# FNet mixing and an MLP-mixer block on one core: rewriting the sine/cosine table stage, loading the first input early, and re-splitting one eviction

## The chip, the cores and the metric

One core of a Trainium2 chip runs the whole program. The metric is the device time of one execution in microseconds (us). Medians are quoted; several runs of one kernel agree within about 0.3%. The profile calls TensorE PE, its weight loads PEld, VectorE DVE, ScalarE ACT and GpSimd POOL.

## The reference, cut to what matters

```python
def _attn_ref(x):                       # x: (8, 3008, 256) float32
    X = np.fft.fft(x, axis=1)           # along the 3008 rows
    X = np.fft.fft(X, axis=2)           # along the 256 columns
    return X.real.astype(np.float32)

def _moe_ref(x, w_tok1, w_tok2, w_ch1, w_ch2):
    xt = x.transpose(0, 2, 1)
    h = np.maximum(xt @ w_tok1, 0.0) @ w_tok2          # token mixing, 3008 -> 256 -> 3008
    u = x + h.transpose(0, 2, 1)
    h2 = np.maximum(u @ w_ch1, 0.0) @ w_ch2            # channel mixing, 256 -> 1536 -> 256
    return (u + h2).astype(np.float32)
```

The Fourier transform along the rows is done as matrix products with a table of cosines and one of sines. The kernel makes these tables on the chip at its start: 24 blocks of 128 rows, 753 useful columns each (padded to 768), stored as fp16. It then treats the 8 batches one after the other.

## The kernel before: the parts that matter

Tables, pass 1: for each of 24 blocks, sine and cosine of 256 columns in fp32. Pass 2: casts to fp16, and angle addition for the other 512 columns.

```python
    def sincos(m, W, Sf, out_sin, out_cos):
        v = ...;  v = m * (1/Sf) + 2**23          # DVE
        v = v - 2**23                             # DVE: rounded quotient
        r = v * (-Sf) + m                         # DVE, two tensors: remainder
        out_sin = Sin(r * 2*pi/Sf)                # ACT
        m4 = m * 4 + Sf                           # DVE
        v2 = m4 * (1/(4*Sf)) + 2**23              # DVE
        v2 = v2 - 2**23                           # DVE
        r2 = v2 * (-Sf) + m                       # DVE, two tensors
        out_cos = Sin(r2 * 2*pi/Sf + pi/2)        # ACT
```

(The body above is abbreviated to one line per instruction; each line is one call in the kernel.)

```python
    elC = gen.tile([P, NT, 256], FP32, tag="elC", bufs=1)
    elS = gen.tile([P, NT, 256], FP32, tag="elS", bufs=1)
    for nt in range(NT):                                             # pass 1
        m = gen.tile([P, 256], FP32, tag="m256")
        nc.vector.tensor_scalar(out=m[:], in0=jrow[:], scalar1=nval[:, nt:nt + 1], ...)
        sincos(m, 256, float(S), elS[:, nt, :], elC[:, nt, :])
    for nt in range(NT):                                             # pass 2
        nc.vector.tensor_copy(out=tabC[:, nt, 0:256], in_=elC[:, nt, :])
        nc.vector.tensor_copy(out=tabS[:, nt, 0:256], in_=elS[:, nt, :])
        for q in (1, 2):
            # tmp1 = elS * ss_q (ACT);  tabC[q] = elC * sc_q - tmp1 (DVE)
            # tmp2 = elC * ss_q (ACT);  tabS[q] = elS * sc_q + tmp2 (DVE)
            ...
```

The pool of the per-batch tiles is opened after the table pool is closed, so that it takes over its memory; the input of batch 0 is loaded inside the batch loop, by 48 loads that POOL issues:

```python
    perb = ctx.enter_context(tc.tile_pool(name="perb", bufs=1))
    work = ctx.enter_context(tc.tile_pool(name="work", bufs=1))
    for b in range(BB):
        x16 = perb.tile([P, NT, D], FP16, tag="x16")
        for nt in range(NT):
            nc.gpsimd.dma_start(out=x16[0:nw, nt, :], ...)           # even rows
            nc.gpsimd.dma_start(out=x16[64:64 + nw, nt, :], ...)     # odd rows
        ...
        for mt in range(2):
            for tbl, dt_, dr in ((tabC, ATt, ATr), (tabS, BTt, BTr)):    # four DFT groups
                pe_lo = pst("pe_lo"); pe_hi = pst("pe_hi")           # 4 of 8 PSUM banks
                po_lo = pst("po_lo"); po_hi = pst("po_hi")
                for nt in range(NT):
                    # 4 matmuls: even and odd rows, columns 0:512 and 512:768 of block nt
                    ...
                # eviction: pos <- po_lo, po_hi (ACT), then eight adds and subtracts (DVE)
```

In the order of the program there are four such DFT groups a batch: group 0 (cosines, left half of the columns), 1 (sines, left), 2 and 3 (right half). The kernel's PSUM pool has eight tiles and a group takes four, so two groups can be open at once. The other place that the change touches is the eviction of the channel mixing's first product, 12 tiles to a step:

```python
                    if ct % 2 == 0:
                        nc.scalar.activation(out=c1[:, ct, :], in_=pc[:], func=AFT.Relu)
                    else:
                        nc.vector.tensor_scalar(out=c1[:, ct, :], in0=pc[:], ..., op0=AT.max)
```

## Time and profile before

| | before |
|---|---|
| time, median of the first 4 runs | 1103.73 us (1103.7 to 1104.23) |
| first matmul | 105.8 us |
| eviction of batch 0's last DFT group starts | 151.9 us |
| batch 0's last matmul ends | 242.75 us |
| one batch after that | 122.3 us |

Start with the page's picture of the span: each digit is the busy share, in tenths, of one of 40 slices of 27.6 us.

```profile
## 2 busy tenths in 40 slices
PE   0001999999999999999999999999999999999998
PEld 0000477666766666665776676666767676666765
DVE  9997176544865367535855367545755466536654
ACT  4585032321333142321323032312332033313232
POOL 2002644000800062001700062003500080000000
```

PE is idle for almost four slices and full after that; DVE is full while PE is idle. The next view gives busy time by stretches: start:end, length, then busy us (and instructions) of PE, PEld, DVE, ACT and POOL, then the recorded clock of PE, the DMA share and GB/s.

```profile
0.00:51.00 51.00, 0.00 (x0) 0.00 (x0) 49.84 (x207) 24.50 (x53) 6.88 (x16) 1.00 0.57 92
51.00:98.00 47.00, 0.00 (x0) 0.00 (x0) 47.00 (x143) 40.17 (x94) 0.00 (x0) 1.00 0.00 0
98.00:103.00 5.00, 0.00 (x0) 0.00 (x0) 4.43 (x17) 1.81 (x4) 0.29 (x1) 1.00 0.00 0
103.00:152.00 49.00, 43.56 (x386) 25.47 (x387) 11.62 (x30) 2.75 (x8) 24.85 (x48) 0.97 0.31 33
```

The four lines are pass 1, pass 2, the small tables for the column transform, and the DFT of batch 0. In the last one POOL is busy issuing the loads. The waits up to 160 us say who waited for whom, in total, how often and longest:

```profile
PE pe_lo L219 <- DMA x<-in_x_dram: 106.4, 3, 105.8
```

PE's first matmul did wait for the input, whose first load was issued at 103.6 us (the timeline puts POOL's wait before it down to ACT's last table instruction, which frees the memory). PE then follows the loads. The timeline of the ACT evictions shows when each of the four DFT groups of batch 0 was done:

```profile
131.00 0.60 ACT L228 ACTIVATE pos<-po_lo 128x512 f16<-128x512 f32 x1 [27.96 <-PE po_lo L223]
...
136.23 0.60 ACT L228 ACTIVATE pos<-po_lo 128x512 f16<-128x512 f32 x1 [4.36 <-PE po_lo L223]
...
144.08 0.60 ACT L228 ACTIVATE pos<-po_lo 128x512 f16<-128x512 f32 x1 [6.99 <-issue]
...
151.88 0.60 ACT L228 ACTIVATE pos<-po_lo 128x512 f16<-128x512 f32 x1 [6.93 <-issue]
```

The last two groups are 7.8 us apart, which is a group at PE's full rate (the four of batch 1 are 7.8 us apart too); the first two wait for loads. Finally, the chain of waits gives the batch period: the last run of channel-mixing matmuls of batch 0, and that of batch 7.

```profile
237.51 5.24 PE pc L362 x48
...
1093.43 5.25 PE pc L362 x48
```

One more reading is needed, of what an instruction costs on an engine. An instruction's duration includes latency that its successor can overlap (on DVE one of 0.28 us is followed after 0.20); what counts is the interval from start to start in a full stretch. In the table passes these intervals are, for 256 fp32 columns: DVE with one tensor 0.20 us (0.26 with a per-partition factor), DVE with two tensors 0.34 (0.40 with a per-partition factor), ACT 0.40 with a per-partition factor.

### The profile page before, as it was taken

The numbers are of one execution on the slowest core, as the hardware profiler recorded it, in microseconds if no ns is written. First come the engines' busy times: TensorE is split into PE (matmuls) and PEld (weight loads), VectorE is DVE, ScalarE is ACT, GpSimd is POOL, SyncE is SP. The second block draws the span as 40 slices with busy tenths as digits, with TensorE's granted clock in tenths as the row PEclk, the third lists the DMA queues.
The fourth block names the chain that finished last, engine by engine and source line by source line (L and its number), as shares of the span: only waits on it lengthen the run. The fifth ranks groups of instructions, "written<-read, shape, count | busy, mean of one in ns | idle before, by whom it ended". The sixth has DMA issues, their size and how long they took to land.

```text
span 1102.7 us, 20768 instructions
## 1 busy us (share of the span) xinstructions
PE 979.7 (89%) x8448; PEld 667.3 (61%) x8448; DVE 669.1 (61%) x1588; ACT 343.6 (31%) x711; POOL 203.8 (18%) x401
## 2 busy tenths in 40 slices
PE   0001999999999999999999999999999999999998
PEld 0000477666766666665776676666767676666765
DVE  9997176544865367535855367545755466536654
ACT  4585032321333142321323032312332033313232
POOL 2002644000800062001700062003500080000000
PEclk9999999999999999999999999999999999999999
DMA  9001423110511032110411032111311041100011
GB/s 168 2 0 12 45 30 48 43 52 1 58 39 57 19 38 40 55 40 11 49 53 43 19 40 46 48 38 18 41 56 54 5 51 45 45 32 1 16 43 56
DMA packets 62415, 42.99 MB, mean 39 GB/s; under 512 B 9105, under 2 KB 61808, under 8 KB 62320
## 3 DMA queue, kind: packets, MB, share of 16 engines
q0 software_dynamic: 35392, 17.01, 13.3%
q1 hardware_dynamic: 26928, 24.65, 6.7%
q8 instruction: 66, 1.08, 0.4%
q14 instruction: 29, 0.24, 0.1%
HBM read 33.98 MB, written 24.64 MB: 53 GB/s over the span
## 4 chain that ended last, share of the span: by engine, by line
PE 73%; DVE 17%; issue 7%; POOL 2%; ACT 1%; DMA 0%; DVEq 0%; ACTq 0%; POOLq 0%
PE pc L362 23%; PE pc L342 22%; PE pe_lo L219 11%; PE pe_hi L221 5%; PE pt L302 4%; PE pU L282 3%; PE pU L278 3%; DVE Yr L316 3%; DVE tabS L151 2%; DVE tabC L144 2%; DVE Yh L316 2%; DVE UTh L330 1%; DVE r L111 1%; DVE r L98 1%; POOL x L191 1%
## 5 line engine op out<-in xcount | busy, mean ns | idle before, releaser
L346 ACT ACTIVATE c<-pc 128x512 f16<-128x512 f32 x288 | 171.9, 597 | 364.5 <-PE pc L342 186.4
L362 PE MATMUL pc<-wc,c 128*128 128x256 f16 x2304 | 259.4, 273 | 0.0
L191 POOL DMA_DIRECT2D x<-in_x_dram x192 | 138.0, 718 | 613.6 <-PE po_hi L225 604.9
L362 PEld LDWEIGHTS <-c 128*128 128x128 f16 x2304 | 225.0, 98 | 36.8
L349 DVE TENSOR_SCALAR c<-pc 128x512 f16<-128x512 f32 x288 | 195.4, 690 | 51.9 <-PE pc L342 48.7
L219 PE MATMUL pe_lo<-tabC,x 64*128 64x512 f16 x384 | 129.6, 384 | 106.8 <-DMA x<-in_x_dram 106.4
L219 PEld LDWEIGHTS <-x 64*128 64x128 f16 x768 | 72.4, 94 | 195.7 <-issue 107.9
L342 PEld LDWEIGHTS <-wc 128*128 128x128 f16 x1152 | 112.2, 98 | 129.7 <-issue 5.9
L195 POOL DMA_DIRECT2D x<-in_x_dram x192 | 139.3, 726 | 2.7 <-issue 2.7
L342 PE MATMUL pc<-UTh,wc 128*128 128x512 f16 x576 | 130.8, 379 | 1.4
L223 PE MATMUL po_lo<-tabC,x 64*128 64x512 f16 x384 | 129.7, 384 | 1.7 <-DMA x<-in_x_dram 1.5
L342 PE MATMUL pc<-UTr,wc 128*128 128x512 f16 x576 | 128.2, 379 | 0.0
L219 PE MATMUL pe_lo<-tabS,x 64*128 64x512 f16 x384 | 127.1, 379 | 0.0
L223 PE MATMUL po_lo<-tabS,x 64*128 64x512 f16 x384 | 126.6, 378 | 0.0
L228 ACT ACTIVATE pos<-po_lo 128x512 f16<-128x512 f32 x32 | 19.1, 597 | 283.2 <-PE po_hi L225 139.5
L221 PE MATMUL pe_hi<-tabC,x 64*128 64x256 f16 x384 | 105.0, 273 | 0.0
L225 PE MATMUL po_hi<-tabC,x 64*128 64x256 f16 x384 | 105.0, 273 | 0.0
L221 PE MATMUL pe_hi<-tabS,x 64*128 64x256 f16 x384 | 103.8, 270 | 0.0
L225 PE MATMUL po_hi<-tabS,x 64*128 64x256 f16 x384 | 103.8, 270 | 0.0
L367 DVE TENSOR_TENSOR osb<-pc,Yr 128x256 f32<-128x256 f32 x96 | 40.7, 424 | 78.6 <-PE pc L362 78.6
L367 DVE TENSOR_TENSOR osb<-pc,Yh 128x256 f32<-128x256 f32 x96 | 40.8, 425 | 76.8 <-PE pc L362 76.8
L232 DVE TENSOR_TENSOR ATt<-pe_lo,pos 128x512 f16<-128x512 f32 x16 | 11.1, 692 | 117.8 <-ACT pos L228 117.8
(101 smaller groups left out, 1286.6 us busy)
## 6 DMA issues: line engine op xcount, KB each, us to landing
out_dram<-osb SPq DMA_DIRECT2D x176, 128.0 KB, 1.7
x<-in_x_dram POOLq DMA_DIRECT2D x368, 32.0 KB, 2.3
wc<-in_moe_w_ch_dram POOLq DMA_DIRECT2D x2, 768.0 KB, 20.6
w2f<-in_moe_w_tok_dram POOLq DMA_DIRECT2D x1, 1504.0 KB, 16.0
out_dram<-osb SPq DMA_DIRECT2D x8, 97.0 KB
w1h<-in_moe_w_tok_dram POOLq DMA_DIRECT2D x1, 768.0 KB, 7.8
out_dram<-osb SPq DMA_DIRECT2D x8, 95.0 KB
w1r<-in_moe_w_tok_dram POOLq DMA_DIRECT2D x1, 704.0 KB, 10.2
```

Of the source, the lines that this page charges most:

```text
L191: nc.gpsimd.dma_start(out=x16[0:nw, nt, :], in_=bass.AP(tensor=x_t, offset=(b * S + nt * P) * D, ap=[[2 * D, nw], [1, D]]))
L195: nc.gpsimd.dma_start(out=x16[64:64 + nw, nt, :], in_=bass.AP(tensor=x_t, offset=(b * S + nt * P + 1) * D, ap=[[2 * D, nw], [1, D]]))
L219: nc.tensor.matmul(pe_lo[:], lhsT=lhs_e, rhs=tbl[0:64, nt, 0:512], start=st, stop=sp)
L221: nc.tensor.matmul(pe_hi[:, 0:256], lhsT=lhs_e, rhs=tbl[0:64, nt, 512:KHP], start=st, stop=sp)
L223: nc.tensor.matmul(po_lo[:], lhsT=lhs_o, rhs=tbl[64:P, nt, 0:512], start=st, stop=sp)
L225: nc.tensor.matmul(po_hi[:, 0:256], lhsT=lhs_o, rhs=tbl[64:P, nt, 512:KHP], start=st, stop=sp)
L316: nc.vector.tensor_tensor(out=Yt[:, kt, :], in0=Yt[:, kt, :], in1=ph[:, 0:D], op=AT.add)
L342: nc.tensor.matmul(pc[:], lhsT=wc1[:, dt, ct * P:(ct + 1) * P], rhs=UTt[:, dt, kc * 512:(kc + 1) * 512], start=(dt == 0), stop=(dt == 1))
L346: nc.scalar.activation(out=c1[:, ct, :], in_=pc[:], func=AFT.Relu)
L349: nc.vector.tensor_scalar(out=c1[:, ct, :], in0=pc[:], scalar1=0.0, scalar2=None, op0=AT.max)
L362: nc.tensor.matmul(pc2[:, 0:D], lhsT=c1[:, ct, ks * P:(ks + 1) * P], rhs=wc2[:, ct, :], start=(ct == 0), stop=(ct == NKT - 1))
L367: nc.vector.tensor_tensor(out=osb[0:hi, :], in0=pc2[0:hi, 0:D], in1=Ut[0:hi, kt, :], op=AT.add)
```

## The change

Its intent is a shorter front. It has four parts:

1. The pool of the per-batch tiles is opened before the table pool, so that it has memory of its own, and batch 0 is loaded first.
2. The two table passes become one loop over blocks, with small buffers in place of two big ones.
3. Table arithmetic: the rounding multiply-add moves to ACT, and the cosine is made as 1 - 2 sin(x/2)^2 from the same remainder, which saves the second range reduction.
4. The channel-mixing evictions are split 8 to 4 between ACT and DVE in place of 6 to 6.

```diff
+    perb = ctx.enter_context(tc.tile_pool(name="perb", bufs=1))
+    def load_x(b):  ...                       # as in the loop before
+    x16_first = load_x(0)
     with tc.tile_pool(name="tgen", bufs=3) as gen:
@@ (cut: sincos gets a variant with multiply-adds on ACT, which no caller uses;
@@  the small tables move ahead of the loop) @@
-        elC = gen.tile([P, NT, 256], FP32, tag="elC", bufs=1)
-        elS = gen.tile([P, NT, 256], FP32, tag="elS", bufs=1)
         for nt in range(NT):
             m = ...
-            sincos(m, 256, float(S), elS[:, nt, :], elC[:, nt, :])
-        for nt in range(NT):
-            nc.vector.tensor_copy(out=tabC[:, nt, 0:256], in_=elC[:, nt, :])
-            nc.vector.tensor_copy(out=tabS[:, nt, 0:256], in_=elS[:, nt, :])
+            elC = gen.tile([P, 256], FP32, tag="elC")
+            elS = gen.tile([P, 256], FP32, tag="elS")
+            va = gen.tile([P, 256], FP32, tag="sv256")
+            nc.scalar.activation(out=va[:], in_=m[:], func=AFT.Copy,
+                                 scale=1.0 / S, bias=TWO23)
+            nc.vector.tensor_scalar(out=va[:], in0=va[:], scalar1=-TWO23, ..., op0=AT.add)
+            r = gen.tile([P, 256], FP32, tag="sr256")
+            nc.vector.scalar_tensor_tensor(out=r[:], in0=va[:], scalar=-float(S),
+                                           in1=m[:], op0=AT.mult, op1=AT.add)
+            nc.scalar.activation(out=elS[:], in_=r[:], func=AFT.Sin, scale=2 * pi / S)
+            nc.scalar.activation(out=h[:], in_=r[:], func=AFT.Sin, scale=pi / S)
+            nc.scalar.activation(out=h2[:], in_=h[:], func=AFT.Square)
+            nc.vector.tensor_scalar(out=elC[:], in0=h2[:], scalar1=-2.0,
+                                    scalar2=1.0, op0=AT.mult, op1=AT.add)
+            nc.vector.tensor_copy(out=tabC[:, nt, 0:256], in_=elC[:])
+            nc.vector.tensor_copy(out=tabS[:, nt, 0:256], in_=elS[:])
             for q in (1, 2):                  # angle addition as before
@@ (cut) @@
-    perb = ctx.enter_context(tc.tile_pool(name="perb", bufs=1))
     for b in range(BB):
-        x16 = perb.tile(...)                  # and its 48 loads
+        x16 = x16_first if b == 0 else load_x(b)
@@ (cut) @@
-                    if ct % 2 == 0:
+                    if ct % 3 != 2:
```

More of the change, by code (lines that the diff above doesn't have):

```diff
@@ L87, with load_x @@
     wc2 = const.tile([P, NKT, D], FP16, tag="wc2")
-    with tc.tile_pool(name="tgen", bufs=3) as gen:
-        def sincos(m, W, Sf, out_sin, out_cos):
-            v = gen.tile([P, W], FP32, tag=f"sv{W}")
-            nc.vector.tensor_scalar(out=v[:], in0=m[:], scalar1=1.0 / Sf,
-                                    scalar2=TWO23, op0=AT.mult, op1=AT.add)
-            nc.vector.tensor_scalar(out=v[:], in0=v[:], scalar1=-TWO23,
+    perb = ctx.enter_context(tc.tile_pool(name="perb", bufs=1))
+    def load_x(b):
+        x16 = perb.tile([P, NT, D], FP16, tag="x16")
+        nc.vector.memset(x16[:, NT - 1, :], 0.0)
+        for nt in range(NT):
+            nw = 64 if nt < NT - 1 else 32
+            nc.gpsimd.dma_start(
+                out=x16[0:nw, nt, :],
+                in_=bass.AP(tensor=x_t, offset=(b * S + nt * P) * D,
+                            ap=[[2 * D, nw], [1, D]]))
+            nc.gpsimd.dma_start(
+                out=x16[64:64 + nw, nt, :],
+                in_=bass.AP(tensor=x_t, offset=(b * S + nt * P + 1) * D,
+                            ap=[[2 * D, nw], [1, D]]))
+        return x16
@@ new lines @@
+    qjr = const.tile([P, NT * 2], FP32, tag="qjr")
+    nc.gpsimd.iota(qjr[:], pattern=[[0, NT], [256, 2]], base=256,
+                   channel_multiplier=0, allow_small_or_imprecise_dtypes=True)
+    dcols = []
+    for dt in range(2):
+        dcol = const.tile([P, 1], FP32, tag=f"dcol{dt}")
+        nc.gpsimd.iota(dcol[:], pattern=[[0, 1]], base=128 * dt,
+                       channel_multiplier=1,
+                       allow_small_or_imprecise_dtypes=True)
+        dcols.append(dcol)
@@ new lines, with sincos @@
+    x16_first = load_x(0)
+    with tc.tile_pool(name="tgen", bufs=3) as gen:
+        def sincos(m, W, Sf, out_sin, out_cos, split):
+            va = gen.tile([P, W], FP32, tag=f"sv{W}")
+            if split:
+                nc.scalar.activation(out=va[:], in_=m[:], func=AFT.Copy,
+                                     scale=1.0 / Sf, bias=TWO23)
+            else:
+                nc.vector.tensor_scalar(out=va[:], in0=m[:], scalar1=1.0 / Sf,
+                                        scalar2=TWO23, op0=AT.mult, op1=AT.add)
+            nc.vector.tensor_scalar(out=va[:], in0=va[:], scalar1=-TWO23,
@@ L96, in sincos @@
                                     scalar2=None, op0=AT.add)
             r = gen.tile([P, W], FP32, tag=f"sr{W}")
-            nc.vector.scalar_tensor_tensor(out=r[:], in0=v[:], scalar=-Sf,
+            nc.vector.scalar_tensor_tensor(out=r[:], in0=va[:], scalar=-Sf,
                                            in1=m[:], op0=AT.mult, op1=AT.add)
@@ L102, in sincos @@
             m4 = gen.tile([P, W], FP32, tag=f"sm{W}")
-            nc.vector.tensor_scalar(out=m4[:], in0=m[:], scalar1=4.0, scalar2=Sf,
-                                    op0=AT.mult, op1=AT.add)
-            v2 = gen.tile([P, W], FP32, tag=f"sw{W}")
-            nc.vector.tensor_scalar(out=v2[:], in0=m4[:], scalar1=1.0 / (4 * Sf),
-                                    scalar2=TWO23, op0=AT.mult, op1=AT.add)
-            nc.vector.tensor_scalar(out=v2[:], in0=v2[:], scalar1=-TWO23,
+            vb = gen.tile([P, W], FP32, tag=f"sw{W}")
+            if split:
+                nc.scalar.activation(out=m4[:], in_=m[:], func=AFT.Copy,
+                                     scale=4.0, bias=Sf)
+                nc.scalar.activation(out=vb[:], in_=m4[:], func=AFT.Copy,
+                                     scale=1.0 / (4 * Sf), bias=TWO23)
+            else:
+                nc.vector.tensor_scalar(out=m4[:], in0=m[:], scalar1=4.0,
+                                        scalar2=Sf, op0=AT.mult, op1=AT.add)
+                nc.vector.tensor_scalar(out=vb[:], in0=m4[:],
+                                        scalar1=1.0 / (4 * Sf), scalar2=TWO23,
+                                        op0=AT.mult, op1=AT.add)
+            nc.vector.tensor_scalar(out=vb[:], in0=vb[:], scalar1=-TWO23,
                                     scalar2=None, op0=AT.add)
             r2 = gen.tile([P, W], FP32, tag=f"sp{W}")
-            nc.vector.scalar_tensor_tensor(out=r2[:], in0=v2[:], scalar=-Sf,
+            nc.vector.scalar_tensor_tensor(out=r2[:], in0=vb[:], scalar=-Sf,
                                            in1=m[:], op0=AT.mult, op1=AT.add)
@@ L117 @@
         ss_q = const.tile([P, NT * 2], FP32, tag="ss_q")
-        qjr = gen.tile([P, NT * 2], FP32, tag="qjr", bufs=1)
-        nc.gpsimd.iota(qjr[:], pattern=[[0, NT], [256, 2]], base=256,
-                       channel_multiplier=0, allow_small_or_imprecise_dtypes=True)
         mq = gen.tile([P, NT * 2], FP32, tag="mq", bufs=1)
@@ L124 @@
         nc.vector.tensor_tensor(out=mq[:], in0=qjr[:], in1=nval_b, op=AT.mult)
-        sincos(mq, NT * 2, float(S), ss_q[:], sc_q[:])
-        elC = gen.tile([P, NT, 256], FP32, tag="elC", bufs=1)
-        elS = gen.tile([P, NT, 256], FP32, tag="elS", bufs=1)
+        sincos(mq, NT * 2, float(S), ss_q[:], sc_q[:], False)
+        for dt in range(2):
+            dcol = dcols[dt]
+            md = gen.tile([P, 256], FP32, tag="m256")
+            nc.vector.tensor_scalar(out=md[:], in0=jrow[:], scalar1=dcol[:],
+                                    scalar2=None, op0=AT.mult)
+            sincos(md, 256, float(D), sdm[:, dt, :], cdm[:, dt, :], False)
         for nt in range(NT):
@@ L133 @@
                                     op0=AT.mult)
-            sincos(m, 256, float(S), elS[:, nt, :], elC[:, nt, :])
-        for nt in range(NT):
-            nc.vector.tensor_copy(out=tabC[:, nt, 0:256], in_=elC[:, nt, :])
-            nc.vector.tensor_copy(out=tabS[:, nt, 0:256], in_=elS[:, nt, :])
+            elC = gen.tile([P, 256], FP32, tag="elC")
+            elS = gen.tile([P, 256], FP32, tag="elS")
+            va = gen.tile([P, 256], FP32, tag="sv256")
+            nc.scalar.activation(out=va[:], in_=m[:], func=AFT.Copy,
+                                 scale=1.0 / S, bias=TWO23)
+            nc.vector.tensor_scalar(out=va[:], in0=va[:], scalar1=-TWO23,
+                                    scalar2=None, op0=AT.add)
+            r = gen.tile([P, 256], FP32, tag="sr256")
+            nc.vector.scalar_tensor_tensor(out=r[:], in0=va[:], scalar=-float(S),
+                                           in1=m[:], op0=AT.mult, op1=AT.add)
+            nc.scalar.activation(out=elS[:], in_=r[:], func=AFT.Sin,
+                                 scale=float(2 * np.pi / S))
+            h = gen.tile([P, 256], FP32, tag="sw256")
+            nc.scalar.activation(out=h[:], in_=r[:], func=AFT.Sin,
+                                 scale=float(np.pi / S))
+            h2 = gen.tile([P, 256], FP32, tag="sp256")
+            nc.scalar.activation(out=h2[:], in_=h[:], func=AFT.Square)
[3 more added lines that the diff above has]
+            nc.vector.tensor_copy(out=tabS[:, nt, 0:256], in_=elS[:])
             for q in (1, 2):
@@ L141 @@
                 tmp1 = gen.tile([P, 256], FP32, tag="tmp1")
-                nc.scalar.activation(out=tmp1[:], in_=elS[:, nt, :], func=AFT.Copy,
+                nc.scalar.activation(out=tmp1[:], in_=elS[:], func=AFT.Copy,
                                      scale=ss_q[:, i:i + 1])
                 nc.vector.scalar_tensor_tensor(
-                    out=tabC[:, nt, c0:c0 + 256], in0=elC[:, nt, :],
+                    out=tabC[:, nt, c0:c0 + 256], in0=elC[:],
                     scalar=sc_q[:, i:i + 1], in1=tmp1[:],
                     op0=AT.mult, op1=AT.subtract)
-                tmp2 = gen.tile([P, 256], FP32, tag="tmp1")
-                nc.scalar.activation(out=tmp2[:], in_=elC[:, nt, :], func=AFT.Copy,
+                tmp2 = gen.tile([P, 256], FP32, tag="tmp2")
+                nc.scalar.activation(out=tmp2[:], in_=elC[:], func=AFT.Copy,
                                      scale=ss_q[:, i:i + 1])
                 nc.vector.scalar_tensor_tensor(
-                    out=tabS[:, nt, c0:c0 + 256], in0=elS[:, nt, :],
+                    out=tabS[:, nt, c0:c0 + 256], in0=elS[:],
                     scalar=sc_q[:, i:i + 1], in1=tmp2[:],
                     op0=AT.mult, op1=AT.add)
-        for dt in range(2):
-            dcol = gen.tile([P, 1], FP32, tag="dcol", bufs=1)
-            nc.gpsimd.iota(dcol[:], pattern=[[0, 1]], base=128 * dt,
-                           channel_multiplier=1,
-                           allow_small_or_imprecise_dtypes=True)
-            md = gen.tile([P, 256], FP32, tag="m256")
-            nc.vector.tensor_scalar(out=md[:], in0=jrow[:], scalar1=dcol[:],
-                                    scalar2=None, op0=AT.mult)
-            sincos(md, 256, float(D), sdm[:, dt, :], cdm[:, dt, :])
         nc.gpsimd.dma_start(out=w1h[:], in_=bass.AP(
@@ L181 @@
             tensor=wc2_t, offset=0, ap=[[D, P], [P * D, NKT], [1, D]]))
-    perb = ctx.enter_context(tc.tile_pool(name="perb", bufs=1))
     work = ctx.enter_context(tc.tile_pool(name="work", bufs=1))
     for b in range(BB):
-        x16 = perb.tile([P, NT, D], FP16, tag="x16")
-        nc.vector.memset(x16[:, NT - 1, :], 0.0)
-        for nt in range(NT):
-            nw = 64 if nt < NT - 1 else 32
-            nc.gpsimd.dma_start(
-                out=x16[0:nw, nt, :],
-                in_=bass.AP(tensor=x_t, offset=(b * S + nt * P) * D,
-                            ap=[[2 * D, nw], [1, D]]))
-            nc.gpsimd.dma_start(
-                out=x16[64:64 + nw, nt, :],
-                in_=bass.AP(tensor=x_t, offset=(b * S + nt * P + 1) * D,
-                            ap=[[2 * D, nw], [1, D]]))
+        x16 = x16_first if b == 0 else load_x(b)
         ATt = perb.tile([P, 2, KTOT], FP16, tag="ATt")
```

## The prediction

> **What bounds it now.** Two parts. Busy time by stretches: from 0 to 103 us PE has no work, DVE is busy 101.3 of 103 us and ACT 66.5; afterwards PE is the limit. The eight batches repeat every (1102.7 - 242.7)/7 = 122.9 us (batch 0's last matmul ends at 242.7 in the chain of waits). The front, from the timeline: table pass 1 takes DVE 1.94 us per block (24 blocks), pass 2 takes 1.98, the small tables 4. Only then are the 48 input loads issued, one every 0.52 us on POOL, 103.6 to 128.5. PE follows the loads, so the last DFT group reaches its eviction at 151.9: 46 us after the first matmul, against 31.5 in batch 1 (four groups, 7.8 us each).
>
> **What the change does.**
> 1. Input load of batch 0 goes first, out of the reused memory. It hides behind table making. Worth about 17 us.
> 2. DVE work per block goes from 3.92 us to: product 0.26, subtract 0.20, remainder 0.34, cosine 0.20, two casts 0.40, four combinations 1.60 = 3.0 us (start-to-start intervals in the timeline).
> 3. ACT per block goes from six activations to eight: four with immediates, four with a per-partition scale. The trace gives 0.40 us start to start for the latter. For immediates I take 0.415 - 0.093 = 0.32 us: 415 ns is the trace's, the Trainium skill, "ScalarE: Activation LUTs", What ACT_TABLE_LOAD costs, gives the overlap of 93 ns (here a 597 ns eviction is followed after 0.50 us, which agrees). Sum 2.88 us. The engines are then nearly balanced, with several handoffs per block; I expect 3.4 us per block, not 3.0.
> 4. Tables become complete block by block, so groups 0 and 1 (eight PSUM banks) follow table making on PE; only groups 2 and 3 remain after it.
> 5. Channel-mixing evictions: ACT 8 of 12, DVE 4. ACT 8 x 0.5 = 4.0 us within 5.18 us of PE. No effect on a PE-bound stage.
> 6. Square might need another table set. The same page, Table sets, says cheap functions are filler in every set (it names relu, copy, identity, abs, not Square); before has one 1.28 us load for Sin, Copy and Relu. I expect one or two loads, not two per block.
>
> **Sum.** Table end T = 1.7 start + 5.2 small tables + 24 x 3.4 + about 1.5 for DVE slowed by POOL issuing = 90 us. After T: about 1 us for the last block, 1.5 for banks, 15.6 for groups 2 and 3, 3 for a PE that was sparsely used and is at half rate at first (before: 604 ns per matmul until 113.6, then 380): 21. Last eviction at 111 instead of 151.9: 41 us gained, all on the critical path. The rest, 951 us, unchanged. 1103.7 - 41 = **1062 us**, range **1050 to 1078**. Chances: faster 0.95, same 0.04, slower 0.01.
>
> **What would show it.** PE's first matmul before 20 us, with tabC and tabS matmuls mixed; table making ending near 90 with both DVE and ACT over 80% busy until then; no long waits for x loads in batch 0; the last DFT eviction near 111; batch period still 122.9 within 0.5; one or two table loads.
>
> **What would make it wrong.** Handoffs between ACT and DVE in a bad static order (4 us per block would cost 14 us: 1077); perfect overlap (3.05: 1053). Group 1 not interleaved with group 0: plus 7 us.  A table load per block: plus 60 us.

## The result

| | before | after |
|---|---|---|
| time, median | 1103.98 us (12 runs) | 1057.59 us (8 runs) |
| first matmul | 105.8 us | 10.6 us |
| tables complete | 98.4 (DFT), 103.0 (all) | 85.9 us |
| eviction of batch 0's last DFT group starts | 151.9 us | 105.0 us |
| batch 0's last matmul ends | 242.75 us | 195.92 us |
| one batch after that | 122.3 us | 122.3 us |

The ratio is 0.9579, 95% interval 0.9569 to 0.9588. Ratios are computed from the mean time of one kernel's fast runs over that of the other's of the same rounds, so they are not quite the ratio of the medians quoted. The change is 46 us faster; the prediction said 1062, with a range of 1050 to 1078.

In the picture of the kernel after (slices of 26.4 us), PE now works in the first three slices, at 3 to 5 tenths:

```profile
## 2 busy tenths in 40 slices
PE   3548999999999999999999999999999999999998
PEld 1115767667666766667666676767666577666665
DVE  9996754367443674358443664446643574436643
ACT  7992343133440434213431324304342133414243
POOL 9300900035000710018000350008000270000000
```

By stretches of the kernel after (columns as before): start and small tables; tables while POOL still issues loads; tables; the last block; and what is left of the DFT.

```profile
0.00:6.00 6.00, 0.00 (x0) 0.10 (x1) 4.80 (x30) 2.55 (x5) 5.43 (x17) 1.00 0.15 16
6.00:40.00 34.00, 15.32 (x76) 4.87 (x76) 33.45 (x109) 30.83 (x86) 28.78 (x49) 1.00 0.76 91
40.00:80.00 40.00, 20.25 (x104) 6.22 (x102) 38.47 (x124) 36.71 (x102) 0.00 (x0) 1.00 0.43 77
80.00:86.00 6.00, 2.86 (x16) 0.97 (x16) 4.60 (x13) 3.58 (x11) 0.00 (x0) 1.00 0.00 0
86.00:105.00 19.00, 18.70 (x195) 13.85 (x194) 11.14 (x24) 2.44 (x6) 0.00 (x0) 1.00 0.01 2
```

DVE is busy for 38.47 of 40 us and ACT for 36.71: both nearly full, as predicted. The wait of PE has changed its cause, from the input to the tables, and is now spread over the 24 blocks:

```profile
PE pe_lo L257 <- DVE tabC L204: 47.2, 24, 10.6
```

The ACT evictions of the four groups: groups 0 and 1 are done together, right after the last table block, and groups 2 and 3 remain.

```profile
85.96 0.60 ACT L266 ACTIVATE pos<-po_lo 128x512 f16<-128x512 f32 x1 [1.07 <-DVE tabS L211]
...
86.71 0.60 ACT L266 ACTIVATE pos<-po_lo 128x512 f16<-128x512 f32 x1
...
97.24 0.60 ACT L266 ACTIVATE pos<-po_lo 128x512 f16<-128x512 f32 x1 [9.65 <-PE po_lo L261]
...
105.04 0.60 ACT L266 ACTIVATE pos<-po_lo 128x512 f16<-128x512 f32 x1 [6.94 <-issue]
```

The last eviction has moved from 151.88 to 105.04, by 46.8 us; the span has shrunk by 1102.7 - 1055.6 = 47.1 us. So the whole gain is made in the front. The chain of waits agrees: (1051.83 - 195.92) / 7 = 122.3 us a batch, unchanged.

```profile
190.68 5.24 PE pc L400 x48
...
1046.58 5.25 PE pc L400 x48
```

One thing in this trace was not expected in detail. The blocks do not come evenly: group 0's first matmul of each block starts 2.33, 2.58 and 4.63 us after the one before, again and again, 9.54 us for three blocks, 3.18 a block. The timeline of ACT shows why there is a longer gap in every third:

```profile
42.83 0.40 ACT L180 ACTIVATE va<-m 128x256 f32<-128x256 f32 x1
44.05 0.42 ACT L187 ACTIVATE elS<-r 128x256 f32<-128x256 f32 x1 [0.82 <-DVE r L185]
...
51.76 1.01 ACT L180 ACTIVATE va<-m 128x256 f32<-128x256 f32 x3
```

The roundings for three coming blocks stand in ACT's program in one burst (x3 in the last line; the first line is the end of the burst before, cut by the window). ACT then has nothing left to do until DVE has made the first remainder, and waits 0.82 us.

### The profile page after: what moved, and what is told of

It is laid out like the page before. It is cut to its first block, busy times and chain, and to the rows that moved or that the text cites. A ratio compares the mean times of both kernels' runs of the same rounds, so it can differ in the third digit from the quotient of the medians.

```text
span 1055.6 us, 20669 instructions
## 1 busy us (share of the span) xinstructions
PE 993.4 (94%) x8448; PEld 668.8 (63%) x8448; DVE 585.2 (55%) x1396; ACT 387.3 (37%) x855; POOL 206.3 (20%) x401
## 4 chain that ended last, share of the span: by engine, by line
PE 75%; DVE 12%; issue 7%; ACT 5%; POOL 0%; DVEq 0%; ACTq 0%; POOLq 0%
PE pc L400 24%; PE pc L380 23%; PE pe_lo L257 11%; PE pe_hi L259 5%; PE pt L340 4%; PE pU L320 3%; PE pU L316 3%; DVE Yr L354 3%; DVE Yh L354 2%; ACT tmp L202 1%; DVE UTh L368 1%; ACT tmp L209 1%; DVE tabS L211 1%; DVE tabC L204 1%; PE ph L351 1%
## 5 line engine op out<-in xcount | busy, mean ns | idle before, releaser
L384 ACT ACTIVATE c<-pc 128x512 f16<-128x512 f32 x384 | 208.4, 594 | 328.5 <-issue 176.0
L96 POOL DMA_DIRECT2D x<-in_x_dram x192 | 130.0, 677 | 655.6 <-PE po_hi L263 651.5
L387 DVE TENSOR_SCALAR c<-pc 128x512 f16<-128x512 f32 x192 | 132.0, 691 | 113.5 <-PE pc L380 113.5
L257 PE MATMUL pe_lo<-tabC,x 64*128 64x512 f16 x384 | 133.8, 394 | 47.5 <-DVE tabC L204 47.2
L261 PE MATMUL po_lo<-tabC,x 64*128 64x512 f16 x384 | 134.2, 395 | 0.0
L261 PE MATMUL po_lo<-tabS,x 64*128 64x512 f16 x384 | 132.7, 391 | 0.0
L100 POOL DMA_DIRECT2D x<-in_x_dram x192 | 132.1, 688 | 2.7 <-issue 2.7
L257 PE MATMUL pe_lo<-tabS,x 64*128 64x512 f16 x384 | 132.3, 390 | 0.0
L257 PEld LDWEIGHTS <-x 64*128 64x128 f16 x768 | 73.2, 95 | 86.6 <-DMA x<-in_x_dram 4.3
L263 PE MATMUL po_hi<-tabC,x 64*128 64x256 f16 x384 | 107.7, 280 | 0.0
L263 PE MATMUL po_hi<-tabS,x 64*128 64x256 f16 x384 | 106.4, 277 | 0.0
L261 PEld LDWEIGHTS <-x 64*128 64x128 f16 x768 | 72.9, 95 | 51.0 <-issue 45.4
L405 DVE TENSOR_TENSOR osb<-pc,Yh 128x256 f32<-128x256 f32 x96 | 40.8, 425 | 78.6 <-PE pc L400 78.6
L405 DVE TENSOR_TENSOR osb<-pc,Yr 128x256 f32<-128x256 f32 x96 | 40.7, 424 | 78.6 <-PE pc L400 78.6
```

Of the source, the lines that this page charges most:

```text
L96: nc.gpsimd.dma_start(out=x16[0:nw, nt, :], in_=bass.AP(tensor=x_t, offset=(b * S + nt * P) * D, ap=[[2 * D, nw], [1, D]]))
L100: nc.gpsimd.dma_start(out=x16[64:64 + nw, nt, :], in_=bass.AP(tensor=x_t, offset=(b * S + nt * P + 1) * D, ap=[[2 * D, nw], [1, D]]))
L257: nc.tensor.matmul(pe_lo[:], lhsT=lhs_e, rhs=tbl[0:64, nt, 0:512], start=st, stop=sp)
L261: nc.tensor.matmul(po_lo[:], lhsT=lhs_o, rhs=tbl[64:P, nt, 0:512], start=st, stop=sp)
L263: nc.tensor.matmul(po_hi[:, 0:256], lhsT=lhs_o, rhs=tbl[64:P, nt, 512:KHP], start=st, stop=sp)
L387: nc.vector.tensor_scalar(out=c1[:, ct, :], in0=pc[:], scalar1=0.0, scalar2=None, op0=AT.max)
```

## The experiments

Twelve kernels were run. Each was correct. "Fresh" in the table is the changed kernel once more, beside its neighbours on one chip.

| run | what | time, us | ratio to before (95%) |
|---|---|---|---|
| r_after_again | the changed kernel, fresh | 1058.49 | 0.9588 (0.9575 to 0.9601) |
| e3_old_split | changed, old eviction split | 1057.09 | 0.9580 (0.9567 to 0.9593) |
| e1_load_only | before, plus early load | 1076.82 | 0.9753 (0.9740 to 0.9766) |
| e2_tables_only | changed, minus early load | 1088.07 | 0.9855 (0.9842 to 0.9869) |
| e4_late_issue | changed, own memory, load at its old place | 1058.93 | 0.9592 (0.9578 to 0.9606) |
| e5_bufs4 | changed, four buffers | 1057.56 | 0.9581 (0.9567 to 0.9596) |
| e6_split_cos | changed, no half angle | 1059.38 | 0.9597 (0.9583 to 0.9611) |
| e7_old_cos | changed, old arithmetic | 1075.19 | 0.9742 (0.9726 to 0.9759) |
| e9_cast_indep | changed, no dependent cast | 1057.60 | 0.9580 (0.9566 to 0.9594) |
| e10_head_early | changed, block heads earlier | 1052.43 | 0.9535 (0.9521 to 0.9549) |
| e8_direct | all 768 columns directly | 1036.14 | 0.9389 (0.9374 to 0.9405) |
| e12_abs | the same with less work a block | 1028.92 | 0.9317 (0.9302 to 0.9333) |

### The changed kernel again, as a yardstick

Edit: none.

> The changed kernel once more, on the chip of its neighbours, so that their ratios can be set beside its own. Every theory expects a ratio of 0.958 within 0.002 to the kernel before, about 1057.6 us.

Measured: 1058.49 us, ratio 0.9588, which agrees with the first 0.9579 within their intervals. Differences of under about 1.5 us between the runs below are not to be read.

### Which part of the gain is the load, and which the tables?

The theory formed after the result is that two shifts add up: the early load lets PE work under the tables, and the tables end earlier. The rival is the split that the prediction made, 17 us for the load and 24 for the rest.

e1, the kernel before with the early load alone (the input has a small pool of its own, because the whole per-batch pool does not fit beside the two big table buffers):

```diff
+    xpool = ctx.enter_context(tc.tile_pool(name="xpool", bufs=1))
+    def load_x(b):  ...          # the same 48 loads, into xpool
+    x16_first = load_x(0)
     with tc.tile_pool(name="tgen", bufs=3) as gen:
@@
-        x16 = perb.tile([P, NT, D], FP16, tag="x16")     # and its loads
+        x16 = x16_first if b == 0 else load_x(b)
```

> The kernel before with one thing added: the input of batch 0 is loaded first, into memory of its own, so that it does not wait for the table pool. The tables are made as before. Theory (two shifts): with the input there, PE's groups 0 and 1 follow the second table pass (51 to 98 us), which already completes blocks one by one; what is left after the tables is the 19 us that the changed kernel shows, and the eviction of the last DFT group comes at 103.4 + 19.2 = 122.6 us in place of 151.9: 29 us gained, 1074.5 us. Rival (the prediction's split): the load alone is worth the 17 us that it names (pacing 14, start 3), and the overlap of groups 0 and 1 needs the block-by-block tables of the change: 1087 us.

Measured: 1076.82 us, 27.1 us faster than before. The theory said 29, the rival 17: the rival falls. The timeline of PE in this run, cut to the first matmuls of blocks, shows PE following the unchanged second pass, one block every 1.99 us, which is that pass's own pace:

```profile
94.99 0.58 PE L227 MATMUL pe_lo<-tabC,x 64*128 64x512 f16 x1 [0.41 <-DVE tabC L163]
...
96.98 0.58 PE L227 MATMUL pe_lo<-tabC,x 64*128 64x512 f16 x1 [0.41 <-DVE tabC L163]
...
98.97 0.58 PE L227 MATMUL pe_lo<-tabC,x 64*128 64x512 f16 x1 [0.40 <-DVE tabC L163]
```

The last DFT eviction comes at 124.4, against the 122.6 estimated; part of the rest is that the tables end later here (the last ACT table instruction starts at 104.28, against 102.53 before). After its last block PE stands idle for 4.96 us here: groups 0 and 1 hold all eight PSUM tiles, and the first eviction stands behind the small tables in ACT's order. Making the small tables after that eviction was not tried.

e2, the changed kernel without the early load:

```diff
-    perb = ctx.enter_context(tc.tile_pool(name="perb", bufs=1))     # ahead of tgen
-    x16_first = load_x(0)
@@ behind tgen @@
+    perb = ctx.enter_context(tc.tile_pool(name="perb", bufs=1))
-        x16 = x16_first if b == 0 else load_x(b)
+        x16 = load_x(b)
```

> The changed kernel without its early load: the pool of the per-batch tiles stands behind the table pool again, and batch 0 is loaded in the loop. Tables as in the changed kernel. Theory (two shifts): the tables end at about 86 us in place of 103, then come the 48 loads and the 48.9 us from the end of the tables to the last DFT eviction, as before: eviction at about 135, 17 us gained, 1086.8 us. Rival (the prediction's split): the faster tables and their block-by-block order are worth 24 of the 41 us that it summed, so 1080 us or less, 1075 if they bring all that the load does not.

Measured: 1088.07 us, 15.8 us faster than before, against 17 by the theory and 24 or more by the rival. The waits of this run show the old picture again, PE waiting for the input and not for tables:

```profile
PE pe_lo L254 <- DMA x<-in_x_dram: 89.3, 1, 89.3
```

The last DFT eviction starts at 134.64, where the theory said 135. So the load alone gives 27 us, the tables alone 16, together 45 (1103.89 - 1058.49); the two add up within 2.5 us. The larger part of the gain is a matter of where a tile lives.

### Memory, or place in the program?

e4 keeps the memory of its own, but leaves the load at its old place, behind the weights' loads:

```diff
-    x16_first = load_x(0)
-        x16 = x16_first if b == 0 else load_x(b)
+        x16 = load_x(b)
```

> The changed kernel with memory of its own for the first input, but with the load left at its old place in the program (behind the weights' loads). Theory: what held the loads in the kernel before was the memory shared with the table pool, not their place in the program. Here nothing holds them: they are issued from about 7 us on, land before the tables need them for long, and the time is that of the changed kernel within 1.5 us (about 1057.6). Rival: the place in the program decides; then the loads come after the tables and the time is about that of tables alone, 1075 to 1087 us.

Measured: 1058.93 us, the changed kernel's time. PE's first matmul comes only at 29.05 us here (10.6 in the changed kernel) and waits for the input there, because the loads, issued from 7.85 us on, in part wait for the weights' loads to land (17 us in all):

```profile
PE pe_lo L255 <- DMA x<-in_x_dram: 29.1, 1, 29.1
```

But PE has caught up with the tables long before they end (from 43 us on its blocks come with the gaps of the changed kernel), and the first group's eviction starts at 87.11. The rival falls. What held the input in the kernel before was the memory that it shared with the table pool; once it had its own, a start of PE 18 us later cost nothing.

### The eviction split

e3: `if ct % 3 != 2:` back to `if ct % 2 == 0:`, all else as changed.

> The changed kernel with the old split of the channel-mixing evictions (6 of 12 on ACT, 6 on DVE, in place of 8 and 4). Theory: the stage is bound by PE (24 matmuls in 5.18 us), so the split is worth nothing: within 1 us of the changed kernel, batch period 122.8 us in both. Rival: relieving DVE brings something in each of the eight batches, 0.3 to 1 us a batch; then this kernel is 2 to 8 us slower than the changed one.

Measured: 1057.09 us against 1058.49 for the changed kernel in the same rounds, with overlapping intervals. The split is worth nothing that can be seen; the batch period is 122.3 us in both. The stage is bound by PE, as predicted.

### What sets the pace of the tables?

e7, the fused loop with the arithmetic of the kernel before (the block's lines from rounding to cosine replaced by a call):

```diff
-            (rounding, remainder, sine, half-angle sine, square, cosine)
+            sincos(m, 256, float(S), elS[:], elC[:], False)
```

> The changed kernel with the table arithmetic of the kernel before in its fused loop: all range reduction on DVE, 3.92 us of DVE per block against 3.0. Theory: tables end 24 x 0.72 (3.92 less the 3.2 that the changed kernel takes) = 17 us later, near 103, and all of it shows: 1074.9 us, 1072 to 1078, the same as the kernel before with the early load alone. Rival: fusing the two passes is itself worth something (PE starts at 11 us in place of 51): then clearly under the time of the kernel with the early load alone, by 5 us or more.

Measured: 1075.19 us; the two intervals of this run and of e1 overlap (0.9742 and 0.9753). Blocks come every 3.93 us (alternating 3.73 and 4.13), which is the sum of DVE's intervals, 3.92. So the work per block sets the time, and fusing the two passes by itself brings little: 1.6 us here, which the intervals do not separate from nothing. A first matmul at 10.9 us in place of 52.9 is worth nothing when the last one is not earlier.

e6, no half angle, but the multiply-adds on ACT:

```diff
+            sincos(m, 256, float(S), elS[:], elC[:], True)
```

> The changed kernel with the half-angle cosine undone: each block makes its cosine by a second range reduction, with the three multiply-adds on ACT (that path stands in the change but is not used for blocks). Work per block by the measured start-to-start intervals: DVE 0.26 + 2 x 0.20 + 2 x 0.34 + 0.40 + 1.60 = 3.34 us, ACT 4 x 0.31 + 0.40 + 4 x 0.40 = 3.24 us. Theory (the table work per block sets the time): 0.34 us more a block on DVE, 24 blocks, 8 us later: 1065.5 us, 1063 to 1069. Rival: ACT or PE is what sets the pace of the front: within 2 us of the changed kernel.

Measured: 1059.38 us, under 2 us slower than the changed kernel, where the theory said 8. Taken by the numbers set down, the rival won, and the theory's 8 us were wrong; but the trace does not show the rival's cause. Blocks come every 3.33 us here, and the sum of DVE's intervals was 3.34: the estimate of this kernel was right. What was wrong was the other side. The changed kernel needs 3.0 us of DVE a block and takes 3.18. The half angle had saved 0.34 us of DVE work a block and got back only 0.15. Over 24 blocks that is 3.6 us; the end of the loop gives part of it back, as PE's last block follows after 1.98 us here and after 4.36 in the changed kernel.

e5, e9 and e10 look for that lost 0.18.

e5: four buffers in place of three for five tiles of the chain (rounded quotient, remainder, half-angle sine, sine, cosine); the square is written in place, two tiles that only the small tables use go down to one buffer, and the product m stayed at three.

> The changed kernel with four buffers in place of three for the five tiles of the block's chain (rounded quotient, remainder, half-angle sine, sine, cosine); the square is written in place to make room. Theory: a block takes 3.2 us instead of DVE's 3.0 because of handoffs between ACT and DVE, which depth relieves: 3.05 us a block, tables end 3 to 4 us earlier, 1053.5 to 1055 us. Rival: DVE is simply full (97% busy in the table stretch), the waits are the tail of each chain, and depth brings under 1 us.

Measured: 1057.56 us, nothing. The bursts of three are still in ACT's timeline (at 42.80 us, for one), with the same wait of 0.82 us after them. Because m stayed at three buffers, this run does not exclude depth by itself.

e9: the cast of the cosine no longer depends on the instruction before it.

```diff
-            nc.vector.tensor_copy(out=tabC[:, nt, 0:256], in_=elC[:])
+            nc.vector.tensor_scalar(out=tabC[:, nt, 0:256], in0=h2[:], scalar1=-2.0,
+                                    scalar2=1.0, op0=AT.mult, op1=AT.add)
```

> The changed kernel with the fp16 copy of the cosine made from the square directly (the same multiply-add written once more to fp16) in place of a cast of the fp32 cosine. Same number of DVE instructions, but the pair cosine, cast is no longer dependent. Trace of the changed kernel: the cast starts 0.33 us after the cosine when it follows it at once, against 0.20 for independent neighbours. Theory (part of the 0.2 us a block above DVE's own 3.0 are such dependent pairs inside DVE): 0.13 us in some 16 to 24 blocks, 2 to 3 us: 1054.5 to 1055.5 us. Rival (DVE waits for ACT anyway, so that the pair only moves the wait): within 1 us of the changed kernel.

Measured: 1057.60 us, nothing that can be seen; three blocks take 9.43 us in place of 9.54, which over 24 blocks is 0.9 us. The rival was right: in the changed kernel's timeline of DVE the lost 0.54 us of three blocks are two dependent pairs (0.33 from cosine to cast in place of 0.20) and one wait for ACT's square (0.46 from the cast before it to the cosine, in place of 0.20). Here the pairs are gone, but that wait has grown to 0.60.

e10: the head of each block (product, rounding, remainder) is written one block earlier, with the three buffers as they were.

```diff
+        def head(nt):
+            (m, va, va - 2**23, r as before);  return r
+        ahead = [head(0)]
         for nt in range(NT):
-            (m, va, va - 2**23, r)
+            if nt + 1 < NT:
+                ahead.append(head(nt + 1))
+            r = ahead.pop(0)
```

> The changed kernel with the head of each block (product, rounding, remainder) written one block earlier in the program, so that the scheduler gives it precedence. In the changed kernel's trace the roundings on ACT come in bursts of three, once every three blocks, and ACT then waits 0.8 us for the first remainder: four buffers did not change it. Theory (the static order of ACT, not the depth, makes the bubble of about 0.6 us every third block): the bubble goes, 3.0 to 3.1 us a block, 3 to 5 us earlier: 1053 to 1055 us. Rival: the bubble comes back elsewhere, as DVE and ACT are both over 90% full: within 1 us of the changed kernel.

Measured: 1052.43 us, 5 us faster than the changed kernel (ratio 0.9535 against 0.9579 and 0.9588, intervals apart), a little more than the theory's 1053 to 1055. Blocks now come every 2.99 us, which is DVE's own 3.0. The timeline of ACT has one rounding a block, and waits of at most 0.25 us in it where there was one of 0.82:

```profile
45.27 0.49 ACT L209 ACTIVATE tmp<-elS,ss_q 128x256 f32<-128x256 f32 x1
46.01 0.42 ACT L194 ACTIVATE elS<-r 128x256 f32<-128x256 f32 x1 [0.25 <-DVE r L183]
46.34 0.90 ACT L216 ACTIVATE tmp<-elC,ss_q 128x256 f32<-128x256 f32 x2
47.14 0.40 ACT L178 ACTIVATE va<-m 128x256 f32<-128x256 f32 x1
```

So the lost 0.18 us was a matter of order: same work, same buffers, another order. The edit moves the whole head, so DVE's order changed too, and no run separates the two engines. Why the roundings came in bursts is not shown either; it would fit that, written in plain sequence, the rounding for a later block has the lowest precedence when the static order is made, and is put off until nothing else is left. The profile's busy share shows only part of the loss. From 40 to 80 us DVE is busy 38.47 us in the changed kernel (96%) and 39.93 here (nearly 100%):

```profile
40.00:80.00 40.00, 21.40 (x108) 6.64 (x108) 39.93 (x133) 38.62 (x105) 0.00 (x0) 1.00 0.43 78
```

That is 4 points, where the pace differs by 6%. In a dependent pair such as cosine and cast, 0.29 of the 0.33 us count as busy, although 0.20 would do.

### A version that beats both

If the work per block sets the time, less work must show in full. e8 makes all 768 columns of a block at once, with no angle addition and no casts: product in turns, rounding, remainder on DVE; sine, half-angle sine and square on ACT; the last multiply-add writes fp16.

```diff
-            (18 instructions of 256 columns a block)
+            u  = (jrow * nval) * (1/S)               # DVE, 768 columns
+            va = u + 2**23                           # DVE
+            va = (va - 2**23) - u                    # DVE, two tensors
+            tabS = Sin(-2*pi * va)                   # ACT, to fp16
+            h  = Sin(pi * va);  h = Square(h)        # ACT
+            tabC = -2*h + 1                          # DVE, to fp16
```

> The changed kernel with other table arithmetic: all 768 columns of a block made at once by range reduction, one sine, one half-angle sine, square and multiply-add, written to fp16 directly; no angle addition, no casts; seven instructions of 768 columns a block in place of 18 of 256. Range reduction in turns. Estimate from the intervals of the trace for 256 columns (DVE single source 0.20, of which about 0.13 per 256 columns is streaming; two sources 0.34, about 0.27 streaming; ACT 0.31, about 0.21 streaming): DVE 3 x 0.46 + 0.87 = 2.25, ACT 3 x 0.73 = 2.2 us a block. Theory (table work per block sets the time until PE itself is the limit): about 2.4 us a block with handoffs, tables end near 4 + 58 = 63 to 67 in place of 86, and all of it shows: 1036 to 1041 us. Rival: PE, at half rate (1.3 us for a block's eight matmuls), or the first input's loads (one pair per 1.1 to 1.3 us) set the pace before that, or the later stages give it back: 1045 us or more.

Measured: 1036.14 us. Blocks come every 2.33 us in most of the stretch, the last DFT eviction at 83.8. The intervals of 256 columns scaled to 768 gave 2.25 us of DVE: a good estimate. In the picture PE's first slices are fuller:

```profile
PE   4589999999999999999999999999999999999998
```

e12 cuts the work again: the cosine is made as the sine of a quarter turn less the absolute value (the sign bit is cleared on DVE), the rounding add goes to ACT in every second block, and heads stand one block earlier as in e10.

```diff
-            va = u + 2**23                           # DVE, every block
+            va = u + 2**23                           # ACT in odd blocks, DVE in even ones
-            h  = Sin(pi * va);  h = Square(h)        # ACT
-            tabC = -2*h + 1                          # DVE
+            h  = va with the sign bit cleared        # DVE, int32 view
+            tabC = Sin(-2*pi * h + pi/2)             # ACT
```

> The direct tables once more with less work a block: the cosine as the sine of a quarter turn less the absolute value (sign bit cleared on DVE) in place of half-angle sine, square and multiply-add; the rounding add on ACT in every second block; heads of blocks written one block earlier. By the intervals of the direct version: DVE 2.02, ACT 1.92 us a block in place of 2.25 and 2.2. Theory (the table work per block still sets the time, PE needs 1.3 us a block): the direct version took about 2.4 us a block; this one about 2.15, tables end 6 to 7 us earlier, 1028 to 1032 us. Rivals: the bit operation runs at one element a cycle (0.87 us in place of 0.46), then DVE is at 2.4 and the time is that of the direct version, 1035 to 1037; or the loads of the first input (48 issues on POOL until 38 us, slower beside a full DVE) pace the first half, then 1032 to 1035 with waits of PE for the input in the trace.

Measured: 1028.92 us, ratio 0.9317, within the range set down; about 2.1 us a block (PE's first matmul of group 0 starts at 8.73 us for the first block and at 57.83 for the 24th, so 2.13 on average), last DFT eviction at 78.6 us. In a full stretch the instruction after the bit operation starts 0.47 us later (at 47.30 and 47.77 in DVE's timeline), not 0.87 as the first rival had it. The second rival falls too: no matmul's wait ends with an input load (one weight load's does, the first, until 4.5 us). The two direct versions use a remainder in turns, whose rounding adds up to 3.3e-4 to a table entry by a calculation of its own in fp32, of the size of fp16's own rounding; the results were correct.

## Why the prediction was right, point by point

- **What bounds it (right).** Front 103 us without PE, then PE. The batch period did not change (122.3 in both), and all of the gain lies before 105 us. The 122.9 in the prediction included the program's tail; it played no part in the sum.
- **End of the tables, 90 us predicted, 85.9 measured.** The start and small tables took 6.0 us in place of 6.9. The loop took 79.8 (from the first block's product at 6.04 to the end of the last write) against 24 x 3.4 + 1.5 = 83.1. Inside it, a block takes 3.18, not 3.4, so 24 x 3.18 = 76.3; the other 3.5 us (the first and the last blocks, which overlap less with others, and the loads) the sum had not named but for its 1.5. So two errors of opposite sign, 5.3 too much for the pace and about 2 too little for the ends, partly cancel: that the loop's sum came so close is in part luck. The handoff term was there, as predicted, but half its size (0.18 a block over DVE's 3.0), and it went away with another order of the instructions (e10), as the prediction's own "bad static order" had it. The term for DVE slowed by POOL's issuing was over-sized: the first two triples of blocks beside the loads took 9.75 and 9.72 us against 9.54 later, 0.4 us in all, not 1.5 (0.8 in the fresh run of the same kernel; in e1, with other work beside the loads, 1.6).
- **After the tables, 21 us predicted, 19.2 measured** (85.87 to 105.04). Group 2 starts 0.7 us after the last table write, where 2.5 were predicted for last block and banks. From there 18.4 us go by to the last eviction, against 15.6 + 3. The half rate of PE is in the trace: blocks of group 2 take 0.64 us until 91.05 and 0.32 after it, so 4.4 us at half rate, about 2.2 lost. No run took this cost away by itself.
- **Evictions worth nothing (right),** e3.
- **Table loads of ACT (right).** There is one load of 1.28 us in all, also with Square.
- **The sum (right within 4.4 us):** 41 us predicted, 46 measured. Both stretches, before and after the end of the tables, were taken as too long.
- **The split of the credit (wrong).** The prediction put it thus: the early load is "Worth about 17 us", and the overlap of groups 0 and 1 comes because "Tables become complete block by block". The early load alone gives 27 us (e1), the tables alone 16 (e2). The kernel before already completed its tables block by block in pass 2, every 1.98 us from 51 us on; PE could not follow because it had no input. The evidence stood in the profile before: the longest wait of PE, 105.8 us, ends with the input, and none ends with a table. The sum came out right because the overlap was counted once, only under the wrong part.

## What to carry to other kernels

- When an engine starts late, ask which wait ends last and remove that one first: here a tile that shared its memory with a closed pool held up an engine that could have followed work that was already complete.
- Two nearly full engines that feed each other need the right order: here it brought 5 us (e10), where a fourth buffer for five of the tiles brought nothing (e5). Try writing the head of the next block before the body of this one, and compare the time per block with the sum of start-to-start intervals; the busy share shows only part of the difference (96% against nearly 100%).
- An experiment that undoes one part can show too little, when another loss hides that part's gain (e6); read the pace per block in its trace before believing the total.

## What the Trainium skill lacked or had wrong

- "ScalarE: Activation LUTs", What ACT_TABLE_LOAD costs: an activation with immediates as 186 ns + 0.833 ns a column, 93 ns more for a pointer operand, and an overlap of 93 ns between neighbours. Nothing was found wrong here. The runs agree: 400 ns for 256 columns and 833 for 768, 493 with a per-partition scale, neighbours 0.30 to 0.31 us apart.
- The same page, Table sets: the hidden batching unit, has no row for the sine's set and does not name Square among the fillers. In these runs Sin, Copy, Square and Relu shared one load of 1283 ns.
- "DMA: Bandwidth & Descriptors", SWDGE vs HWDGE vs iDMA, says that DVE locks GpSimd out in its 2-port mode while GpSimd writes descriptors; that section gives no size, and no page was found that says what DVE loses. Here DVE lost 0.4 us beside 48 loads in the changed kernel, 0.8 in its fresh run and 1.6 in e1 (13 blocks of pass 1 in 26.9 us, where later ones take 1.94 each). It goes with the issuing more than with the traffic: in the kernel before, from 10 to 30 us, 157 to 213 GB/s were moved with POOL idle, and DVE kept its 1.94. POOL gave way more: from 20 to 30 us it issued 19 loads in the changed kernel, but 14 in e8 and 13 in e12, whose DVE instructions are three times as long. That DVE causes this is a guess; no run separated it.
- "TensorE: Matmul & The Clock Gate", Seeing it yourself, warns that the recorded clock events are unreliable on trn2. The runs agree: from 40 to 80 us the recorded clock is 1.00 in the changed kernel and 0.51 in e4, while the same 64 x 512 matmuls take 0.58 to 0.63 us in both (0.38 to 0.39 at full rate). Durations decide.
- No page was found that says what the order can cost in which the instructions of two nearly full engines are written; it cost 0.19 us a block here (3.18 against 2.99 in e10).
